# Decayed keys of two chunks by two GpSimd operations per unit, and the last output tile cut at column 384

## The chip, the cores and the metric

The kernel runs on one core of a Trainium2 chip. The metric is the device time of one execution in microseconds, taken as the median of several runs. A profiled execution of the kernel has a span (first to last instruction) and a time of its own, which is somewhat longer than the span.

## What is computed

Two stages follow each other: a block-wise linear attention with decay, and a feed-forward layer with a PReLU.

```python
# q, k, v: (4, 8, 768, 64); lam: (8,), between 0.97 and 0.99; block = 64
for b in range(nb):                       # 12 blocks
    intra = einsum('bhic,bhjc->bhij', qb, kb) * Dmask     # Dmask[i, j] = lam ** (i - j), i >= j
    intra = einsum('bhij,bhjd->bhid', intra, vb)
    inter = einsum('bhid,bhde->bhie', qb * lam_pow, kv_state)
    out[:, :, sl] = intra + inter
    kb_dec = kb * rev_pow                 # lam ** (63 - j): the decayed keys
    kv_state = lam_block * kv_state + einsum('bhsd,bhse->bhde', kb_dec, vb)

x = out as (3072, 512)
h = x @ w_in                              # (512, 2048)
g = maximum(h, 0) + alpha * minimum(h, 0)
return g @ w_out                          # (2048, 512) -> (3072, 512) float32
```

## The kernel before

**Chunks and units.** The 3072 rows are cut into six chunks of 512. A chunk holds two batches of 256 positions each; chunk `c` belongs to positions `256 * (c // 2)` and up. The attention of a chunk is done in four units: a batch (`bi`) and a half of the heads (`hh`, four heads). There are 24 units, `units[n] = (c, bi, hh)`. In chunks 0 to 3 (`c < FIRST`, `FIRST = 4`) a partition holds two neighbouring positions, and a state is carried over 128 positions. In chunks 4 and 5 the positions lie in order, each partition holds positions 128 apart (`e` = 0 and 1), and the state is carried over `N = 64`.

**A unit's steps.** Keys, and queries from unit 12 on, come as float32 by SP's DMAs (`kraw`, `qraw`), values as float16 by GpSimd's DMAs (`vh`). `cast` makes float16 copies (`qk16`). From unit 12 on, `turn_by_dma` has SP issue a transposing DMA that writes `qkT`. `decayed` multiplies the turned queries with their decay (`qdT`, L494). `key_decayed` multiplies the raw keys with theirs (`kdec`): L444 in chunks 0 to 3, L437 in chunks 4 and 5. `cluster` (L506 and on) is TensorE's part: scores (`s`, L586), new states from `kdec` and the values (L603), and the outputs of the unit before from the states (L538) and the masked scores (L558). `state` and `aged` carry the state on (L666, L677, L686).

**The feed-forward part.** `up` multiplies with `w_in` (L705), ScalarE takes the negative part (L716), VectorE joins the two (`gate`, L728), `down` multiplies with `w_out` (L738), and `store` (L749, L753) copies a 128x512 output tile from PSUM to SBUF on ScalarE and issues its DMA on ScalarE's queue. The tiles of the last chunk are made after everything else by `down_last` (L760), sixteen matmuls of 128x128 weights for each piece.

**Order.** Every engine works through its own instructions in program order; the order is written out by hand up to the second chunk's end, and then made by `weave`, which alternates the attention steps of chunk `c + 1` with the matmuls of chunk `c`. For unit `x` the four steps are `turns`, `joined`, `first_states` and `further_states`. `turns(x)` issues the transposing DMA of unit `x + 1`, at times the loads of the next chunk, and `decayed(x)`; `first_states(x)` ages the state and casts the keys of unit `x + 2` (GpSimd) and its queries (ScalarE); `further_states(x)` ends with `key_decayed(x + 2)` on GpSimd. So GpSimd's order in this part is: decayed queries of `x`, cast of keys of `x + 2`, decayed keys of `x + 2`, decayed queries of `x + 1`. Keys are decayed two units ahead of the cluster that reads them, into four buffers (`kdec`, `bufs=4`). The output tiles go to three buffers (`osb`, `bufs=3`).

Of the kernel before, what the change touches and what calls it, by code (L numbers as in the profile page):

```python
# [11 lines left out]
def kernel(  # L12
# [22 lines left out]
    ALU = mybir.AluOpType  # L35

    B, H, S, D = q.shape
# [3 lines left out]
    NC = (S // W) * 2  # L41
    NHP = H // 2
    DM = H * D
# [20 lines left out]
        out=lam_sb,  # L64
# [5 lines left out]
    raws = {}  # L70
# [4 lines left out]
    FIRST = 4  # L75
# [37 lines left out]
    w_out_sb = const.tile([128, NF, DM], fp16, name="w_out_sb")  # L113
# [50 lines left out]
    kdecay = const.tile([128, H, 2], fp32, name="kdecay")  # L164
# [8 lines left out]
    nkdecay = const.tile([128, H], fp32, name="nkdecay")  # L173
# [192 lines left out]
    def bank(slot, name):  # L366
        return ps.tile([128, CH], fp32, tag=f"b{slot}", name=name)
# [30 lines left out]
    def engine(x):  # L398
        return nc.vector if x == "V" else nc.gpsimd

    def view(t, hh):
        return t[:, ds(4 * hh, 4), :].rearrange("p h (e d) -> p e h d", e=2)
# [29 lines left out]
    def key_decayed(n, eng="G"):  # L432
        c, bi, hh = units[n]
        kr = view(raws[c, bi, "k"], hh)
        kdec = half_pool.tile([128, 2, 4, D], fp16, tag="kdec", name="kdec", bufs=4)
        if c >= FIRST:
            engine(eng).tensor_tensor(  # L437
                out=kdec.rearrange("p e h d -> p h e d"),
                in0=raws[c, bi, "k"][:, ds(4 * hh, 4), :].rearrange("p h (e d) -> p h e d", e=2),
                in1=nkdecay[:, ds(4 * hh, 4)].unsqueeze(2).unsqueeze(3).to_broadcast([128, 4, 2, D]),  # L440
                op=ALU.mult,
            )
        for e in range(2 if c < FIRST else 0):
            engine(eng).tensor_tensor(  # L444
                out=kdec[:, e],
                in0=kr[:, e],
                in1=kdecay[:, ds(4 * hh, 4), e].unsqueeze(2).to_broadcast([128, 4, D]),
                op=ALU.mult,
            )
        T.setdefault(n, {})["kdec"] = kdec  # L450
# [295 lines left out]
    def store(c, t, c0=0, n=DM):  # L746
        o_ps = O.pop((c, t))
        o_sb = o_pool.tile([128, DM], fp32, tag="osb", name="o_sb")
        nc.scalar.activation(o_sb[:, 0:n], o_ps[:, 0:n], AF.Copy)  # L749
        pb, b = c // 2, 2 * (c % 2) + t % 2  # L750
        rows = out[ds(b * S + pb * W, W), ds(c0, n)]
        rows = rows.rearrange("(j e) d -> e j d" if c < FIRST else "(e j) d -> e j d", e=2)[t // 2]
        nc.scalar.dma_start(out=rows, in_=o_sb[:, 0:n])  # L753

    def down_last(c, t, nc_parts):
        n = DM // nc_parts
        for x in range(nc_parts):
            o_ps = O[c, t] = bank(TURN[(t + x) % 3], "o_ps")
            for f in range(NF):
                nc.tensor.matmul(  # L760
                    o_ps[:, 0:n],
                    lhsT=G[c, f][:, t // 2, t % 2, :],
                    rhs=w_out_sb[:, f, ts(x, n)],
                    start=(f == 0),
                    stop=(f == NF - 1),
                )
            store(c, t, x * n, n)

# [35 lines left out]
    load_win(256, 256)  # L806
    query_decay()
    key_decayed(0, "V")
    turn(0)
    decay_mask(1)  # L810
    key_decayed(1, "G")
    fill(6)
    turned(0, "V")
# [18 lines left out]
    turned(1, "A")  # L832
    masked(0, 0)
    key_decayed(2, "G")
    masked(0, 1)
    cast(2, "k", "A")
# [424 lines left out]
        moe = ups[:1] + [x for f in range(1, NF) for x in (ups[f], downs[f - 1])] + downs[-1:]  # L1261
        weave(att, moe)
    for t in range(4):
        down_last(NC - 1, t, 1 if t < 3 else 2)


# [28 lines left out]
```

## Time and profile before

| | |
|---|---|
| median of 3 runs | 221.33 us (219.97 to 222.4) |
| profiled execution: time | 221.9 us |
| profiled execution: span | 220.1 us |
| mean granted TensorE clock | 0.988 |
| HBM read, written | 27.28 MB, 6.29 MB |
| largest groups: L705, L738 on TensorE | 98.1 and 81.2 us |
| L728 on VectorE, L716 on ScalarE | 73.2 and 59.0 us |
| all `kdec` operations on GpSimd | 30 of 128x256, 18.4 us; 8 of 128x512, 8.3 us |

PE is TensorE's matmuls, PEld its weight loads (which overlap the matmuls), DVE is VectorE, ACT ScalarE, POOL GpSimd, SP SyncE; a name with a q is that engine's issuing of DMAs. A group's row has the line, the engine and operation, what is written and read with shapes and types, the count, and then busy us, mean ns of one, idle us before, and what ended that idle time. A timeline's row begins with start and duration in us. The rows of slices cut the span into 40 equal parts; a digit is the busy share in tenths. The chain that ended last is followed back from the last instruction, at each step to what released it. Ends of matmuls are modelled, so the distance between starts says more than a duration.

### The profile page before, as it was taken

To read this page: it belongs to the slowest core of one execution; us is meant where nothing else is said; L and a number is where in the kernel's file an instruction comes from. 1 tells how busy PE (TensorE), PEld (TensorE's weight loads), DVE (VectorE), ACT (ScalarE), POOL (GpSimd) and SP (SyncE) were. 2 spreads that over 40 slices of the span, in tenths; PEclk is the share of its full clock that TensorE was granted. 3 is DMA by queue.
4 is the path that set the end of the run, shared out by engine and by line. 5 is a ranking of instruction groups with operands and counts; after the bars stand their busy time and mean duration, and the time that the engine had idled before them with its cause. 6 is when DMAs were issued, how large, how long until landed. Compare 5 with 4: busy or idle time off the path is not lost.

```text
span 220.1 us, 5893 instructions
## 1 busy us (share of the span) xinstructions
PE 211.8 (96%) x2463; PEld 114.6 (52%) x2463; DVE 127.1 (58%) x260; ACT 111.6 (51%) x209; POOL 95.9 (44%) x146
## 2 busy tenths in 40 slices
PE   8988899899999999999999999999999999999992
PEld 8777544556665545454545444444444444444461
DVE  3988577666887787464667566556755254443000
ACT  4762585744655564646664545555445434443120
POOL 7874796553998770776596243620100000000000
PEclk9999699999999999999999999999999999999998
DMA  4999999999998599299269995236011001100221
GB/s 118 244 193 232 192 159 183 202 171 196 299 229 199 85 219 118 74 184 172 74 89 217 180 229 130 64 82 71 27 51 48 17 35 48 48 38 13 95 92 53
DMA packets 71194, 28.44 MB, mean 129 GB/s; under 512 B 52080, under 2 KB 68224, under 8 KB 71168
## 3 DMA queue, kind: packets, MB, share of 16 engines
q0 software_dynamic: 26592, 8.65, 35.6%
q1 hardware_dynamic: 40800, 13.11, 31.0%
q10 hardware_dynamic: 3776, 6.31, 8.0%
q8 instruction: 19, 0.31, 0.6%
q14 instruction: 7, 0.06, 0.1%
HBM read 27.28 MB, written 6.29 MB: 153 GB/s over the span
## 4 chain that ended last, share of the span: by engine, by line
PE 91%; ACT 2%; DVE 2%; POOL 2%; issue 1%; POOLq 0%
PE h_ps L705 38%; PE o_ps L738 32%; PE o_ps L760 6%; PE acc L538 3%; PE s L586 2%; PE op_fill L380 2%; PE acc L558 2%; PE tp L466 2%; PE tp L461 1%; PE acc L603 1%; ACT qkT L392 1%; PE mk_ps L267 1%; POOL vh L83 0%; PE s L603 0%; DVE less L245 0%
## 5 line engine op out<-in xcount | busy, mean ns | idle before, releaser
L728 DVE SCALAR_TENSOR_TENSOR g<-m,oma,h_ps 128x512 f16<-128x512 f32 (+1 forms) x106 | 73.2, 696 | 64.9 <-ACT m L716 63.5
L705 PE MATMUL h_ps<-xT,w_in_sb 128*128 128x512 f16 (+1 forms) x424 | 98.1, 364 | 0.2
L716 ACT ACTIVATE m<-h_ps 128x512 f32<-128x512 f32 (+1 forms) x106 | 59.0, 557 | 57.4 <-PE h_ps L705 55.5
L738 PE MATMUL o_ps<-w_out_sb,g 128*128 128x512 f16 x320 | 81.2, 379 | 0.0
L705 PEld LDWEIGHTS <-w_in_sb 128*128 128x128 f16 x424 | 40.4, 99 | 41.1 <-issue 1.2
L738 PEld LDWEIGHTS <-g 128*128 128x128 f16 x320 | 30.9, 98 | 35.8
L749 ACT ACTIVATE o_sb<-o_ps 128x512 f32<-128x512 f32 (+1 forms) x25 | 14.5, 580 | 18.8 <-PE o_ps L760 11.1
L619 DVE TENSOR_TENSOR sm<-s,dmask 128x512 f16<-128x512 f32 x32 | 21.2, 683 | 1.8 <-PE s L586 1.8
L392 ACT ACTIVATE xT<-acc 128x512 f16<-128x512 f32 x22 | 13.1, 597 | 16.8 <-PE acc L558 9.6
L686 POOL TENSOR_TENSOR old<-R,rdecay 128x128 f32<-128x128 f16 x24 | 9.6, 408 | 26.3 <-DVE R L677 15.7
L444 POOL TENSOR_TENSOR kdec<-kraw,kdecay 128x256 f16<-128x256 f32 x30 | 18.4, 638 | 1.5 <-DMA kraw<-in_k_dram 0.8
L494 POOL TENSOR_TENSOR qdT<-qkT,nqdecay 128x512 f16<-128x512 f16 x8 | 9.3, 1165 | 21.5 <-DMA qkT<-qk 17.8
L494 POOL TENSOR_TENSOR qdT<-qkT,qdecay 128x512 f16<-128x512 f16 (+1 forms) x12 | 12.0, 1003 | 6.0 <-ACT qkT L392 3.0
L760 PE MATMUL o_ps<-w_out_sb,g 128*128 128x512 f16 (+1 forms) x80 | 14.0, 336 | 0.0
L380 PE MATMUL op_fill<-filler 128*128 128x128 f16 x122 | 10.7, 258 | 1.1 <-DVE sel L203 1.1
L538 PE MATMUL acc<-qdT,R 64*64 64x64 f16 (+1 forms) x216 | 10.9, 217 | 0.9 <-ACT R L675 0.7
L760 PEld LDWEIGHTS <-g 128*128 128x128 f16 x80 | 7.8, 98 | 6.2
L538 PEld LDWEIGHTS <-R 64*64 64x64 f16 x224 | 5.9, 104 | 9.5 <-issue 6.3
L666 DVE SCALAR_TENSOR_TENSOR R<-R,nrdecay,s 128x64 f16<-128x64 f16 x48 | 10.4, 275 | 0.0
L380 PEld LDWEIGHTS <-filler 128*128 128x128 f16 x122 | 9.3, 119 | 1.6 <-DVE sel L203 1.1
L586 PE MATMUL s<-qkT 64*64 64x128 f16 (+1 forms) x384 | 9.3, 210 | 0.9 <-issue 0.5
L558 PE MATMUL acc<-sm,vh 64*64 64x128 f16 (+1 forms) x352 | 8.5, 211 | 0.0
(98 smaller groups left out, 159.5 us busy)
## 6 DMA issues: line engine op xcount, KB each, us to landing
out_dram<-o_sb ACTq DMA_DIRECT2D x23, 256.0 KB, 2.1
kraw<-in_k_dram SPq DMA_DIRECT2D x12, 256.0 KB, 5.1
kraw<-in_k_dram SPq DMA_DIRECT2D x6, 512.0 KB, 8.0
qraw<-in_q_dram SPq DMA_DIRECT2D x10, 256.0 KB, 6.6
vh<-in_v_dram POOLq DMA_DIRECT2D x8, 256.0 KB, 9.4
w_out_sb<-in_moe_w_out_dram POOLq DMA_DIRECT2D x4, 512.0 KB, 8.3
w_in_sb<-in_moe_w_in_dram POOLq DMA_DIRECT2D x3, 512.0 KB, 10.4
qh<-in_q_dram POOLq DMA_DIRECT2D x5, 256.0 KB, 9.0
```

Source lines behind the costliest of these rows:

```text
L380: nc.tensor.matmul(t[:, 0:128], lhsT=filler, rhs=filler, start=True, stop=True)
L392: nc.scalar.activation(out, in_, AF.Copy)
L444: engine(eng).tensor_tensor(out=kdec[:, e], in0=kr[:, e], in1=kdecay[:, ds(4 * hh, 4), e].unsqueeze(2).to_broadcast([128, 4, D]), op=ALU.mult,
L494: engine(eng).tensor_tensor(out=out, in0=src, in1=(qdecay if c < FIRST else nqdecay)[:, hh].rearrange("p e h j -> p (e h) j").unsqueeze(2) ...
L538: nc.tensor.matmul(o, lhsT=before[ds(hl * 64, 64), hp, :], rhs=x, start=not own and e == 0, stop=False, skip_group_check=True,)
L619: nc.vector.tensor_tensor(out=t["sm"][hl], in0=t["s"][:, hl].rearrange("p (h x j) -> p h x j", h=2, x=2), in1=mask_of(hl, hh), op=ALU.mult,)
L705: nc.tensor.matmul(h_ps[:, 0:n] if bi is None else h_ps[:, 0:n].rearrange("p (e j) -> p e j", e=2), lhsT=w_in_sb[:, gi, ts(f, 128)], rhs=x ...
L716: nc.scalar.activation(m[:, 0:n], HP[c, f, bi][:, 0:n], AF.Relu, scale=-1.0)
L728: nc.vector.scalar_tensor_tensor(out=g, in0=mv, scalar=oma[:, f : f + 1], in1=hv, op0=ALU.mult, op1=ALU.add)
L738: nc.tensor.matmul(O[c, t], lhsT=G[c, f][:, t // 2, t % 2, :], rhs=w_out_sb[:, f, :], start=(f == 0), stop=(f == NF - 1),)
L749: nc.scalar.activation(o_sb[:, 0:n], o_ps[:, 0:n], AF.Copy)
L760: nc.tensor.matmul(o_ps[:, 0:n], lhsT=G[c, f][:, t // 2, t % 2, :], rhs=w_out_sb[:, f, ts(x, n)], start=(f == 0), stop=(f == NF - 1),)
```

## The change

It has two parts. In `key_decayed`, chunks 4 and 5 no longer have an operation of their own over 128x512 elements; all chunks use the loop over `e`, two operations of 128x256 per unit, and the decay is chosen by chunk. In chunks 4 and 5 both halves are multiplied by the same decay. In `down_last`, the widths of the pieces are handed over; the last tile goes out as 384 and 128 columns, where it was 256 and 256.

```diff
         kdec = half_pool.tile([128, 2, 4, D], fp16, tag="kdec", name="kdec", bufs=4)
-        if c >= FIRST:
-            engine(eng).tensor_tensor(
-                out=kdec.rearrange("p e h d -> p h e d"),
-                in0=raws[c, bi, "k"][:, ds(4 * hh, 4), :].rearrange("p h (e d) -> p h e d", e=2),
-                in1=nkdecay[:, ds(4 * hh, 4)].unsqueeze(2).unsqueeze(3).to_broadcast([128, 4, 2, D]),
-                op=ALU.mult,
-            )
-        for e in range(2 if c < FIRST else 0):
+        for e in range(2):
+            decay = kdecay[:, ds(4 * hh, 4), e] if c < FIRST else nkdecay[:, ds(4 * hh, 4)]
             engine(eng).tensor_tensor(
                 out=kdec[:, e],
                 in0=kr[:, e],
-                in1=kdecay[:, ds(4 * hh, 4), e].unsqueeze(2).to_broadcast([128, 4, D]),
+                in1=decay.unsqueeze(2).to_broadcast([128, 4, D]),
                 op=ALU.mult,
             )
...
-    def down_last(c, t, nc_parts):
-        n = DM // nc_parts
-        for x in range(nc_parts):
+    def down_last(c, t, pieces):
+        c0 = 0
+        for x, n in enumerate(pieces):
             o_ps = O[c, t] = bank(TURN[(t + x) % 3], "o_ps")
             for f in range(NF):
                 nc.tensor.matmul(
                     o_ps[:, 0:n],
                     lhsT=G[c, f][:, t // 2, t % 2, :],
-                    rhs=w_out_sb[:, f, ts(x, n)],
+                    rhs=w_out_sb[:, f, ds(c0, n)],
                     start=(f == 0),
                     stop=(f == NF - 1),
                 )
-            store(c, t, x * n, n)
+            store(c, t, c0, n)
+            c0 += n
...
-        down_last(NC - 1, t, 1 if t < 3 else 2)
+        down_last(NC - 1, t, (DM,) if t < 3 else (DM - 128, 128))
```

## The prediction

> **What bounds the kernel now.** I read the page first, for the busy engine and for the chain of waits.
>
> ```profile
> span 220.1 us, 5893 instructions
> ...
> PE 211.8 (96%) x2463; PEld 114.6 (52%) x2463; DVE 127.1 (58%) x260; ACT 111.6 (51%) x209; POOL 95.9 (44%) x146
> ...
> POOL 7874796553998770776596243620100000000000
> ...
> PE 91%; ACT 2%; DVE 2%; POOL 2%; issue 1%; POOLq 0%
> ```
>
> TensorE works for 211.8 of 220.1 us, and 91% of the chain that ended last is TensorE's. GpSimd (POOL) has 44%, all in the first three quarters. So an edit on GpSimd counts only if it makes TensorE wait, and an edit at the very end counts in full, since nothing comes after it.
>
> The first edit touches units 16 to 23 (chunks 4 and 5). Their decayed keys are written between 100.4 and 140.9 us. From 95 us on, the list of who waited for whom has not one row for TensorE. How far ahead GpSimd runs is seen in its timeline, start and duration in us, beside the chain in order of time:
>
> ```profile
> 107.27 0.40 POOL L686 TENSOR_TENSOR old<-R,rdecay 128x128 f32<-128x128 f16 x1 [4.67 <-DVE R L677]
> ...
> 108.18 1.04 POOL L437 TENSOR_TENSOR kdec<-kraw,nkdecay 128x512 f16<-128x512 f32 x1
> 109.18 1.16 POOL L494 TENSOR_TENSOR qdT<-qkT,nqdecay 128x512 f16<-128x512 f16 x1
> ...
> 115.34 1.04 POOL L437 TENSOR_TENSOR kdec<-kraw,nkdecay 128x512 f16<-128x512 f32 x1
> ...
> 118.41 1.16 POOL L494 TENSOR_TENSOR qdT<-qkT,nqdecay 128x512 f16<-128x512 f16 x1 [0.26 <-DMA qkT<-qk]
> ```
>
> ```profile
> 109.95 0.12 PE s L603 x12
> ...
> 115.66 0.18 PE acc L538 x8
> 115.85 0.13 PE s L586 x16
> 115.97 0.12 PE s L603 x12
> ```
>
> L603 reads the decayed keys. The keys of unit 16, written from 100.44 to 101.5, are read at 109.95, and those of unit 17, written from 108.18 to 109.2, at 115.97: margins of 8.5 and 6.7 us. The next unit's keys are written at 110.85 and read at 123.65, so the margin grows. The decayed queries of unit 16, which follow the keys of unit 17 on GpSimd, end at 110.3 and are read at 115.66 (L538): 5.3 us, the smallest margin of anything that stands behind a changed operation and is made by GpSimd itself.
>
> The second edit is at the end. Here the timeline of the last tile:
>
> ```profile
> 212.48 0.60 ACT L749 ACTIVATE o_sb<-o_ps 128x512 f32<-128x512 f32 x1 [2.86 <-PE o_ps L760]
> ...
> 214.22 0.38 ACT L749 ACTIVATE o_sb<-o_ps 128x256 f32<-128x256 f32 x1 [1.15 <-PE o_ps L760]
> 214.64 0.34 ACTq L753 DMA_DIRECT2D out_dram<-o_sb  x1
> 215.97 0.38 ACT L749 ACTIVATE o_sb<-o_ps 128x256 f32<-128x256 f32 x1 [1.36 <-PE o_ps L760]
> 216.38 0.34 ACTq L753 DMA_DIRECT2D out_dram<-o_sb  x1
> ```
>
> After the last matmul come a copy of 0.38 us, a gap of 0.03, the output's DMA, 1.7 us from issue to landing (216.38 to 218.1), and 2.0 us of closing work up to 220.1.
>
> **Part one: keys by two operations.** Removed: eight operations of 128x512. Added: sixteen of 128x256, of the form that the first four chunks have on the same line pair:
>
> ```profile
> L444 POOL TENSOR_TENSOR kdec<-kraw,kdecay 128x256 f16<-128x256 f32 x30 | 18.4, 638 | 1.5 <-DMA kraw<-in_k_dram 0.8 <-ACT kdecay L292 0.6
> ...
> L437 POOL TENSOR_TENSOR kdec<-kraw,nkdecay 128x512 f16<-128x512 f32 x8 | 8.3, 1041 | 0.0
> ```
>
> The group of 30 has a median of 616 ns, a lowest of 604 and a highest of 848. With the median, one unit costs 2 x 0.616 - 1.041 = 0.19 us more; from below 2 x 0.604 - 1.049 = 0.16, from above 2 x 0.848 - 1.034 = 0.66. I take 0.19, because after 60 us all operations of this form lie within 605 to 619 ns. The sum over eight units is 1.5 us of GpSimd (1.3 to 5.3). Nothing can be gained: the one operation had no wait before it (idle 0.0) and its result is not read sooner.
>
> On the path I cost it at nothing, and the cover is the margins above. Queued behind a unit's keys on GpSimd are the decayed queries of the unit before, the cast of the next unit's keys and, twice, two loads of the values (0.9 us each of issuing). Each of them shifts by 0.2 us, in the tightest stretch (107.3 to 117.2, three changed units, no idle time) by up to 0.6. Against that stand 5.3 us or more. The cast of keys also releases SP's transposing DMA. For units 18 and 19 the queries' cast on ScalarE ends 1.6 and 3.1 us after GpSimd's cast, so this DMA doesn't move; for unit 17 GpSimd had been idle for 4.67 us just before, so the shift of unit 16's keys is used up there. Even where such a DMA moves by 0.2, its median landing of 4.1 us ends about 3 us before TensorE asks for it (unit 20: lands by 135.5, read at 138.7). The new wait of TensorE, for the second half of each unit's keys, ends with the margin of the whole. If the cover were gone, the price would be the 0.2 us of each unit, 1.5 in all, with the dearest rows 5.3.
>
> A row of the trace speaks for the dear end: at 8.4 us VectorE and GpSimd both run this operation, and the two then take 839 and 848 ns, against 426 and 614 apart. In chunks 4 and 5 VectorE's operations (L728, L628, L666) each take one operand from PSUM, and the changed operation kept to 1034 to 1049 ns among them. [...]
>
> **Part two: 384 and 128 columns.** TensorE: the 512-column tiles come 3.46 us apart for 16 matmuls (209.02 to 212.48), 0.216 each; the 256-column pieces 1.74, 0.109 each. 384 columns lie half way, 0.1625, so 2.60 us for sixteen. For 128 columns the nearest rows are:
>
> ```profile
> 18.81 0.95 PE L380 MATMUL op_fill<-filler 128*128 128x128 f16 x14
> ...
> 54.83 0.39 PE L461 MATMUL tp<-ident,k 128*128 128x128 f16 x4
> ```
>
> and, for the weights of this very step (busy us, mean ns, idle us):
>
> ```profile
> L760 PEld LDWEIGHTS <-g 128*128 128x128 f16 x80 | 7.8, 98 | 6.2
> ```
>
> A single one lasts 0.219, so the fourteen started (0.95 - 0.22) / 13 = 0.056 us apart, and the four, each with weights of its own, (0.39 - 0.22) / 3 = 0.057. That is in the proportion of the columns, though a weight load lasts 98 ns: the loads overlap. So sixteen take 0.90 us, and both pieces 3.50 against 3.49 before: TensorE ends 0.01 us later. From above, with 98 ns each, they would take 1.57, which is 0.68 more.
>
> [...] The trace shows 56 in both streams, the one with changing weights being only four long.
>
> ScalarE: the first piece's copy starts at 212.48 + 2.60 = 215.08 and lasts 0.49 (half way between 0.597 and 0.384; the 384-column exponential of L277 takes 0.489). Its DMA is issued from 215.60 to 215.94. The second piece is ready at 215.98, so ScalarE is free just in time; at worst it loses some 0.03. The last copy, 128 columns, takes 0.28 by the same line (0.597 - 3 x 0.107; L675 takes 0.274 for 128 columns): 0.10 us less than 0.38.
>
> The output's DMA: the table of transfers has
>
> ```profile
> out_dram<-o_sb ACTq DMA_DIRECT2D x23, 256.0 KB, 2.1
> ...
> out_dram<-o_sb ACTq DMA_DIRECT2D x2, 128.0 KB, 1.7
> ```
>
> 0.4 us for 128 KB, so 0.2 for the 64 KB that the last transfer loses: 1.5 us. Bounds: 1.7 if it is all fixed, 1.3 if the slope doubles. The 192 KB of the first piece land at 215.60 + 1.9 = 217.5, before the last at 216.29 + 1.5 = 217.8, so they are hidden by 0.3 us; taken as 256 KB (2.1) still by 0.1.
>
> Sum: +0.01 (TensorE) + 0 (keys) - 0.10 (copy) - 0.2 (landing) = -0.3 us, with bounds from -0.5 to +0.6. The profiled execution took 221.9, 1.8 more than its span; that would give 221.6. The median of the three runs is 0.57 below it, so I subtract from 221.33: 221.0.
>
> **The rivals.**
> - *The last sixteen matmuls are paced by their weight loads.* Place: the 128-column piece, from about 215.1 us. It decides as soon as a 98 ns load can't run under a 56 ns matmul. Price +0.68 - 0.3: about +0.4, so 221.7, slower than before. For it: the row of weight loads; against it: the two streams above. Chance 0.09, and the page's 81 ns (+0.1, 221.4) another 0.06.
> - *The transfer is all fixed cost.* Only the copy's 0.10 is gained: 221.2. For it: 1.7 against 2.1 is a small part of either, and medians are rounded. Chance 0.12.
> - *GpSimd's delay reaches TensorE.* If each unit's 0.19 to 0.66 us were paid, +1.5 to +5.3, 222.5 to 226.3. It decides where the shift passes 5.3 us, or 3 us through SP's transposes; 0.6 are expected. Chance 0.05.
>
> **How the numbers follow.** The forecast has the remaining 0.68, and its time is 221.0. All cases but the last lie within 0.5 us of the time before, less than the scatter of its three runs (219.97 to 222.4). So the range is set by that scatter, moved by the forecast at the low end (219.7), and at the high end (222.4) with 0.2 for the paced matmuls and the cheap end of the GpSimd case: 222.6. A measurement of this kernel can tell about 1%, 2.2 us, from no change. Only the dear part of the GpSimd case (0.04) passes it; scatter of a median of few runs adds some 0.05 on each side. Faster 0.05, within 1% 0.86, slower 0.09.
>
> **What would show it.** Right: GpSimd's keys at 0.60 to 0.63 us, sixteen of them; no wait of TensorE from 95 us on; the copies at the end of 0.49 and 0.28 us, starts 0.9 us apart; a landing near 1.5 us; a span near 219.8. Wrong: a wait of L603, L586 or L538 for GpSimd or for a transpose; keys of 0.8 us; starts of the two last copies 1.3 us or more apart (weights); an unchanged 1.7 us landing.

## The result, and the profile after

The changed kernel took 220.27 us (median of 20 runs, 219.52 to 221.08), the kernel before 220.88 (20 runs, 219.97 to 222.4). The ratio is 0.9963 with a 95% interval of 0.9948 to 0.9979: a gain of 0.5 to 1.1 us, 0.8 in the middle; the two medians lie 0.6 apart. The time lies in the forecast range (219.7 to 222.6) and the sign is as predicted, but the gain is two to three times the 0.3 us that was worked out. Ratios here and below leave out executions at a much lower granted clock (0.56 to 0.85), of which there were three, none of them in this comparison.

The two profiled executions differ by more, 218.0 against 220.1 us of span, and most of that is not the change. The page after:

```profile
span 218.0 us, 5901 instructions
...
PE 209.7 (96%) x2463; PEld 112.9 (52%) x2463; DVE 126.9 (58%) x260; ACT 111.4 (51%) x209; POOL 97.4 (45%) x154
...
POOL 7874797655988680875597352720200000000000
```

and the stretch from 20 to 40 us, which the change doesn't touch, first after and then before (busy us and count of each engine, then the granted clock of TensorE, DMA share, GB/s):

```profile
20.00:40.00 20.00, 18.20 (x209) 10.26 (x207) 13.51 (x24) 12.98 (x26) 14.99 (x23) 1.00 1.32 189
```

```profile
20.00:40.00 20.00, 18.56 (x168) 10.23 (x166) 12.71 (x22) 11.97 (x25) 14.35 (x23) 0.91 1.32 188
```

Before, TensorE had a granted clock of 0.91 in this stretch (half speed for 3.4 us of it, by the clock's records), after, 1.00. It got through 168 matmuls there before and 209 after. This comes and goes from run to run in both kernels (six of the changed kernel's 20 executions have a mean clock of 0.992, the others 0.998 to 1.0). So I compare from a place behind it: the start of ScalarE's copy of the third tile of the last chunk, 212.48 us before and 211.01 after. That part, 1.47 us, is start-up scatter and not the change: the first changed operation, unit 16's keys, already starts 1.48 us earlier (98.96 against 100.44). What is left, with differences taken before rounding:

| from the third tile's copy | before | after | difference |
|---|---|---|---|
| start of the last copy | 3.49 | 3.56 | +0.07 |
| its length with the gap up to the DMA | 0.41 | 0.31 | -0.11 |
| DMA, issue to landing | 1.70 | 1.57 | -0.13 |
| closing work, last landing to end | 2.01 | 1.57 | -0.45 |
| sum | 7.62 | 7.01 | -0.62 |

The first three rows are the predicted effect, -0.17 us where -0.3 was worked out. The fourth, the largest, was not predicted at all. The first three can be read from the timeline after (start, duration):

```profile
211.01 0.60 ACT L743 ACTIVATE o_sb<-o_ps 128x512 f32<-128x512 f32 x1 [2.86 <-PE o_ps L754]
...
213.61 0.49 ACT L743 ACTIVATE o_sb<-o_ps 128x384 f32<-128x384 f32 x1 [2.00 <-PE o_ps L754]
214.13 0.34 ACTq L747 DMA_DIRECT2D out_dram<-o_sb  x1
214.57 0.28 ACT L743 ACTIVATE o_sb<-o_ps 128x128 f32<-128x128 f32 x1 [0.47 <-PE o_ps L754]
214.88 0.34 ACTq L747 DMA_DIRECT2D out_dram<-o_sb  x1
```

The fourth is in the closing instructions, which all have the line of the program's last call (L1290 before, L1285 after). The two views of that line, GpSimd's rows alone (lowest, median and highest ns, first and last start):

```profile
L1290 POOLq DRAIN  x3: 107/178/2668, 153.7 to 219.7; - x3
...
L1290 POOLq EVENT_SEMAPHORE_RANGE_CLEAR  x1: 157/157/157, 219.2 to 219.2; - x1
```

```profile
L1285 POOLq DRAIN  x3: 45/98/2678, 152.6 to 217.7; - x3
...
L1285 POOLq EVENT_SEMAPHORE_RANGE_CLEAR  x1: 158/158/158, 217.6 to 217.6; - x1
```

A drain is an instruction of the closing work; GpSimd clears the semaphores and then drains once more. Before, the drain starts 0.5 us after the clearing; after, about 0.2. To the nanosecond, the clearing ended at 219.351 and the drain ran from 219.689 to 219.867 before; after, 217.710 and 217.744 to 217.789. A gap of 0.338 us became 0.034, and a drain of 0.178 became 0.045. The drain names no semaphore in the trace, so it waits for no other engine by what is recorded. In the trace of before an 8 KB transfer on queue q14, whose kind the profile's page calls "instruction", runs from 219.21 to 219.66, and the drain starts 24 ns behind it. That this transfer causes the gap is not borne out: in the trace of after the like transfer runs from 217.59 to 218.13 and outlasts a drain that isn't held.

GpSimd's keys did what was expected of their time:

```profile
L438 POOL TENSOR_TENSOR kdec<-kraw,nkdecay x16: 609/612/618, 99.0 to 139.8; 128x256 f16<-128x256 f32 x16
```

The list of who waited for whom has no row for TensorE's matmuls (PE) from 95 us on, as before. The rows for its weight loads (PEld), 4.6 us in all and 5.0 before, name an issue, VectorE or TensorE itself, and none names GpSimd.

### The profile page after: what moved, and what is told of

It is laid out like the page before. It is cut to its first block, busy times and chain, and to the rows that moved or that the text cites. A ratio compares the mean times of both kernels' runs of the same rounds, so it can differ in the third digit from the quotient of the medians.

```text
span 218.0 us, 5901 instructions
## 1 busy us (share of the span) xinstructions
PE 209.7 (96%) x2463; PEld 112.9 (52%) x2463; DVE 126.9 (58%) x260; ACT 111.4 (51%) x209; POOL 97.4 (45%) x154
## 4 chain that ended last, share of the span: by engine, by line
PE 91%; ACT 2%; DVE 2%; issue 2%; POOL 2%; ACTq 0%; POOLq 0%
PE h_ps L699 37%; PE o_ps L732 32%; PE o_ps L754 6%; PE acc L532 3%; PE s L580 2%; PE op_fill L380 2%; PE acc L552 2%; PE tp L460 2%; PE tp L455 1%; PE acc L597 1%; ACT qkT L392 1%; PE mk_ps L267 1%; ACT xT L392 1%; POOL vh L83 0%; ACT m L710 0%
## 5 line engine op out<-in xcount | busy, mean ns | idle before, releaser
L699 PE MATMUL h_ps<-xT,w_in_sb 128*128 128x512 f16 (+1 forms) x424 | 96.7, 359 | 0.5 <-DVE g L722 0.2
L699 PEld LDWEIGHTS <-w_in_sb 128*128 128x128 f16 x424 | 39.6, 98 | 40.6 <-issue 1.4
L732 PEld LDWEIGHTS <-g 128*128 128x128 f16 x320 | 30.9, 98 | 35.8
L743 ACT ACTIVATE o_sb<-o_ps 128x512 f32<-128x512 f32 (+2 forms) x25 | 14.5, 580 | 18.8 <-PE o_ps L754 11.0
L754 PE MATMUL o_ps<-w_out_sb,g 128*128 128x512 f16 (+2 forms) x80 | 14.0, 336 | 0.0
L754 PEld LDWEIGHTS <-g 128*128 128x128 f16 x80 | 7.2, 98 | 6.9
L438 POOL TENSOR_TENSOR kdec<-kraw,nkdecay 128x256 f16<-128x256 f32 x16 | 9.5, 612 | 0.0
```

Of the source, the lines that this page charges most:

```text
L438: engine(eng).tensor_tensor(out=kdec[:, e], in0=kr[:, e], in1=decay.unsqueeze(2).to_broadcast([128, 4, D]), op=ALU.mult,)
L699: nc.tensor.matmul(h_ps[:, 0:n] if bi is None else h_ps[:, 0:n].rearrange("p (e j) -> p e j", e=2), lhsT=w_in_sb[:, gi, ts(f, 128)], rhs=x ...
L732: nc.tensor.matmul(O[c, t], lhsT=G[c, f][:, t // 2, t % 2, :], rhs=w_out_sb[:, f, :], start=(f == 0), stop=(f == NF - 1),)
L754: nc.tensor.matmul(o_ps[:, 0:n], lhsT=G[c, f][:, t // 2, t % 2, :], rhs=w_out_sb[:, f, ds(c0, n)], start=(f == 0), stop=(f == NF - 1),)
```

## The experiments

Three theories came up in turn. **A**: GpSimd is held once at a fixed place of its instruction stream; the keys' eight more instructions move that place from the closing work to where GpSimd idles anyway. **B**: the closing work is shorter because the last transfer is smaller. **C**, from a surprise on the way: SP is held in the same manner. The expectations call A's hold a fetch, and one of them speaks of fetched blocks: both are suppositions of the author, which no run shows. All closing numbers below are from the profiled execution of each kernel, one for each; ratios are to the kernel before, timed beside it. The kernels with one and with four memsets, the kernel before with one SP instruction, and the changed kernel with two were profiled once and have no ratio.

**One part alone.** The two parts of the diff, each without the other.

> Only the last tile is cut at 384; the keys are as before, so GpSimd has as many instructions as before. Theory A (a fetch for GpSimd during the closing work held the kernel before; its place depends on GpSimd's instruction count): last landing to end stays 2.0 us, GpSimd's last two instructions come after a gap of about 0.34 us, and the gain is that of copy and landing alone, about 0.15 to 0.2 us against before (ratio about 0.999). Theory B (the closing work got shorter because the last transfer is smaller): last landing to end 1.5 us, gain 0.6 us, ratio about 0.997.

> Only the keys by two operations; the last tile is 256 and 256. Theory A: eight more GpSimd instructions, last landing to end 1.5 us instead of 2.0, gain about 0.45 us (ratio about 0.998), TensorE's part up to the last tile unchanged. Theory B: closing work 2.0 us, no gain (ratio 1.000). In both: no wait of TensorE for GpSimd after 95 us.

With the tail alone: ratio 0.9994 (0.9971 to 1.0017), third tile's copy to last landing 5.44 us as in the changed kernel, and the closing work 2.01 as before, with a gap of 0.323 on GpSimd. With the keys alone: ratio 0.9976 (0.9952 to 1.0), 5.61 to the landing as before, and closing work 1.57 with a gap of 0.034. So -0.17 us belongs to the tail and -0.45 to the keys, and the two add up to the whole -0.62. This rests on the traces: the ratios' intervals reach about 0.5 us to each side, and can't tell the two parts from each other. B is out, by the closing work of the two traces. The tail that was meant as the gain is the smaller part; the keys, costed at nothing, are the larger.

**Instructions that do nothing.** Is it the split of the keys, or only the number of GpSimd's instructions?

```diff
+    pad = const.tile([128, 1], fp32, name="pad")
...
         T.setdefault(n, {})["kdec"] = kdec
+        for _ in range(1 if c >= FIRST else 0):
+            nc.gpsimd.memset(pad, 0.0)
```

> The kernel before with one 128x1 memset on GpSimd after each of the eight units' keys of chunks 4 and 5; nothing reads it. Theory A: the count of instructions alone decides, so last landing to end 1.5 us and a gain of about 0.45 us, as with the keys by two operations. Rival (the split of the keys itself does it, by timing): 2.0 us and no gain.

> The changed kernel with the same eight memsets, sixteen GpSimd instructions more than before in all. Theory A: if a fetch is met only when the last instructions stand just behind the end of a fetched block, the closing work stays at 1.5 us and the time that of the changed kernel (within 0.1 us); if the place matters in a finer way, 2.0 us and 0.45 us slower than the changed kernel. Rival (the gain comes from the changed kernel's parts, not from the count): as the changed kernel.

The first was a miss: ratio 1.0003 (0.9984 to 1.0022), closing work 1.86 us. But the gap had moved. It was 0.034 ahead of the drain and 0.334 behind it. The count explains it: these memsets each wait on GpSimd's own semaphore, and nine separate waiting instructions fell away (44 before, 35 here). With eight memsets more and nine waits less, GpSimd had one instruction less, and it was held one instruction later in its closing sequence. The second, the changed kernel with the same memsets (seven more than before in all), stayed at 1.56 us, with a ratio of 0.9979 (0.9958 to 1.0), and the tail's total of 7.00 was that of the changed kernel.

So the count was set cleanly, by memsets without waits behind GpSimd's last work, in the kernel before:

```diff
+    pad = const.tile([128, 16], fp32, name="pad")
...
+    for i in range(8):            # 1 and 4 in the other two
+        nc.gpsimd.memset(pad[:, i : i + 1], 0.0)
     for t in range(4):
         down_last(NC - 1, t, 1 if t < 3 else 2)
```

> The kernel before with eight 128x1 memsets on GpSimd behind its last decayed queries, each into a column of its own, with no wait; nothing reads them. This makes GpSimd's instructions eight more without a change of anything else (in the earlier kernel with memsets, nine separate waits fell away, so it had one instruction less, not eight more). Theory A (count decides): last landing to end 1.56 us, no gap between GpSimd's last clearing of semaphores and its last drain, gain 0.45 us as with the keys by two operations. Rival (the split of the keys decides): 2.0 us with the gap of 0.34, no gain.

> One such memset. Theory A: the gap of 0.34 us is met one instruction earlier, between GpSimd's drain and the clearing of the semaphores, and last landing to end is still 1.9 to 2.0 us. Rival: gap where it was before.

> Four such memsets. Theory A: the gap moves ahead of GpSimd's first closing instructions, where GpSimd waits for SP anyway, so it is hidden in part or whole: last landing to end 1.56 us, or up to 1.9 if the fetch begins only when the last semaphore arrives. Rival: 2.0 us.

Eight memsets: closing work 1.57 us, ratio 0.9974 (0.9951 to 0.9997), the gain of the keys without any change of the keys. Four: 1.57. One: 1.88, with the gap of 0.335 between GpSimd's drain and the clearing, one instruction earlier than before. Measured on the trace of each, in instructions against the kernel before:

```
GpSimd instructions                   gap of GpSimd in its closing work       landing to end, us
-1 (before, memsets at the keys)      0.334 behind the last drain             1.86
 0 (before; tail alone)               0.338, 0.323 ahead of the last drain    2.01, 2.01
+1 (one memset at the end)            0.335 ahead of the clearing             1.88
+4 (four memsets at the end)          none                                    1.57
+7 (changed, memsets at the keys)     none                                    1.56
+8 (eight at the end; keys; changed)  none                                    1.57
```

In the views, eight memsets first, then one, the clearing follows 0.1 us behind the drain, or 0.5 us:

```profile
L1293 POOLq DRAIN  x2: 45/72/98, 217.3 to 217.6; - x2
...
L1293 POOLq EVENT_SEMAPHORE_RANGE_CLEAR  x1: 157/157/157, 217.4 to 217.4; - x1
```

```profile
L1293 POOLq DRAIN  x2: 45/76/107, 217.7 to 218.4; - x2
...
L1293 POOLq EVENT_SEMAPHORE_RANGE_CLEAR  x1: 157/157/157, 218.2 to 218.2; - x1
```

The place moves by one instruction for each that is added: A is shown as far as the place goes. Counted in the traces, the held instruction is GpSimd's 197th in each row that has a gap. In the changed kernel the 197th is an operation on decayed queries at 143.51 us, and it does start late: 0.38 us behind the wait ahead of it, where the same operation took 0.09 before. So the hold is still there, at a place where TensorE doesn't wait for it. The case of none added is dearer than its neighbours by 0.14 us, mostly because its last drain takes 0.178 instead of 0.045; why, was not tried.

**The last copy on VectorE.** In the changed kernel's chain of waits ScalarE's DMA issue stands just ahead of the last copy:

```profile
213.61 0.50 ACT o_sb L743
214.11 0.02 issue
214.13 0.34 ACTq L747
214.47 0.04 issue
214.51 0.02 ACTq L743
214.53 0.04 issue
214.57 0.28 ACT o_sb L743
```

The last matmul ended at 214.47; in the other tiles ScalarE follows within 0.04 us, here after 0.10, since it was issuing the 384 columns' DMA until 214.47 and then took one more wait. The edit:

```diff
-        nc.scalar.activation(o_sb[:, 0:n], o_ps[:, 0:n], AF.Copy)
+        last = c == NC - 1 and t == 3 and c0 > 0
+        copy_on("V" if last else "A", o_sb[:, 0:n], o_ps[:, 0:n])
...
-        nc.scalar.dma_start(out=rows, in_=o_sb[:, 0:n])
+        (nc.sync if last else nc.scalar).dma_start(out=rows, in_=o_sb[:, 0:n])
```

> The changed kernel with the last copy (128 columns) on VectorE and its DMA on SP's queue. In the changed kernel ScalarE was free only after the first piece's copy, DMA issue and a semaphore, 0.07 us after TensorE's end as worked out. If that wait is real: from the third tile's copy to the last landing 5.37 us or less instead of 5.44, and a gain of 0.05 to 0.1 us; GpSimd's count is that of the changed kernel, so the closing work stays at 1.56. Rival: VectorE's copy is slower than 0.28 us or SP's issue dearer than 0.34, and it is no gain.

The rival was right on the landing: 5.46 us against 5.44. VectorE began its copy 0.09 us after the last matmul, took 0.29, and SP's issue was 0.02 longer. Yet the closing work, expected to stay at 1.56, fell to 1.14 us, and the ratio was 0.9906 (0.9881 to 0.9931), the best of all. Where SP had taken 0.48 us from the wait that the last landing ends to its next wait, whose semaphore had long arrived, it now took 0.06. The trace explains 1.03 us of the gain over the kernel before, a ratio of 0.995; the rest of the 0.9906 is not explained. It comes from five runs with mean clocks of 0.998 to 1.0, while seven of the 17 runs of the kernel before stood at 0.992.

**SP's count.** Was that SP's own issue of the last DMA, or once more one instruction more?

```diff
+    nc.sync.wait_ge(apart, 1)     # long reached; twice in the third kernel
     for t in range(4):
```

> The changed kernel with one more instruction on SP, a wait on a semaphore that has long had its value, behind SP's last transposing DMA. In the changed kernel SP takes 0.48 us from the wait that the last landing ends to the next one, whose semaphore had nothing left to come; in the kernel with the last copy on VectorE that step took 0.06. Theory C (SP too is held once at a fixed place of its instruction stream, so that one instruction more puts it ahead of the last landing, where it is hidden): closing work 1.12 to 1.15 us instead of 1.57, gain 0.4 us on the changed kernel, ratio to before about 0.994. Rival D (the step is shorter because the last DMA was issued by SP): 1.57 us, as the changed kernel.

> The kernel before with the same one SP instruction. Theory C: SP's step 0.06 to 0.08 us instead of 0.47; GpSimd's gap of 0.34 stays, so closing work about 1.6 us instead of 2.0. Rival D: 2.0 us.

> The changed kernel with two such SP instructions. Theory C: the hold moves one more instruction ahead, and is hidden there too: closing work 1.12 to 1.15 us. Rival D: 1.57 us.

With one SP instruction the changed kernel took 219.23 us, ratio 0.9926 (0.9899 to 0.9953); SP's step is 0.09 and the closing work 1.17. The first and last start of SP's two waits, in the changed kernel and then with one instruction more:

```profile
L1285 SPq EVENT_SEMAPHORE  x2: 28/28/28, 216.5 to 216.9; - x2
```

```profile
L1287 SPq EVENT_SEMAPHORE  x2: 28/28/28, 216.5 to 216.6; - x2
```

With two, 0.07 and 1.14. In the kernel before, one makes SP's step 0.09, leaves GpSimd's gap at 0.337, and the closing work is 1.61; that run's last landing took 1.95 us instead of 1.70, so its time says nothing more. C holds, D is out.

**Neither part of the change.** The kernel before, with four memsets on GpSimd and one SP wait.

> Neither part of the change: the kernel before with four memsets behind GpSimd's last work and one SP wait that is already met. Theories A and C: no hold on either engine, closing work 1.12 to 1.15 us; third tile's copy to the end 5.61 + 1.13 = 6.74 us, against 7.62 before and 7.01 with the change; ratio to before about 0.996, as good as the changed kernel or better by some 0.25 us. Rival D: 1.57 us, 7.18.

Ratio 0.9929 (0.9902 to 0.9956): five instructions that compute nothing gained at least as much as the change (0.9963, 0.9948 to 0.9979; the intervals just overlap). Its profile was taken while TensorE had a granted clock of 0.56, so of it only the closing work is used, 1.15 us, and not the tail's total of 6.74. That is 0.86 us less than before, a ratio of 0.996; the timed one comes from five runs, and its surplus is not explained. The versions with the best ratios are the changed kernel with one SP instruction or with the last copy on VectorE; their intervals overlap with each other and with this one.

## Why the prediction was right, and where it was wrong

**What bounds the kernel.** Right. GpSimd works 1.5 us more (97.4 against 95.9), and TensorE waits for it nowhere from 95 us on, where the changed operations stand.

**Keys, their price.** Right: 0.612 us each where 0.616 was taken, sixteen of them, and margins that hid it. The dear end (0.848, both engines at it at once) was not met; the highest was 0.618.

**Keys, "Nothing can be gained".** Wrong, and the step that failed. It looked at waits and readers alone, and took the 2.0 us behind the last landing as a constant. The instruction count moved it: -0.45 us, shown by the keys alone and by eight idle memsets in their place.

**TensorE's last pieces.** Right, and closely: the starts in the trace are 0.1625 us apart for 384 columns and 0.056 for 128, both as taken. The groups by shape have this row for the sixteen (busy us, mean ns, idle us):

```profile
L754 PE MATMUL o_ps<-w_out_sb,g 128*128 128x128 f16 x16 | 1.1, 219 | 0.0
```

(1.06 - 0.219) / 15 = 0.056, each with weights of its own, whose loads take 98 ns. The rival of matmuls paced by weight loads is out for these sixteen. No run shows the 81 ns that the prediction gives a chance of 0.06, nor the +0.1 us drawn from it: this stream kept to 56 ns through all sixteen.

**The copy.** 0.277 us as taken (0.28), but it began 0.07 later than before where 0.01, at worst some 0.03 more, was allowed. The worked-out time left out one further wait of ScalarE, behind its DMA issue.

**The landing.** The right mechanism with the wrong size: -0.13 us instead of -0.2. The slope came from medians of 2.1 and 1.7 us; the third tile's own 256 KB landed in 2.03 us before, which would have given 0.16 for 64 KB. The rival of a fully fixed transfer is out as well: the last 64 KB on ScalarE's queue landed in 1.57 to 1.58 us in all five versions that have them, the last 128 KB in 1.70 to 1.71 in seven of eight (1.95 in the eighth).

So the tail gave 0.17 of the 0.3 us expected, and a mechanism that no rival held gave 0.45 more. The time fell within the range, but most of the gain came from where none was expected: that the total gain was no smaller than forecast is luck.

**What stays open.** What the hold is, a fetch or something else, is not shown. The traces show a fixed count, 197 for GpSimd and 80 for SP, and an 8 KB transfer on q14 that follows each hold seen in the closing work. It starts 0.69 to 0.72 us behind the start of GpSimd's held instruction in all five traces that have the gap (220.38 us before). Where the gap is gone, one such transfer more runs at 144 to 156 us instead (at 242 in the profile at 0.56 of the clock). Behind SP's held instruction one starts 0.63 to 0.82 us later (219.21 before, the one that ends 24 ns ahead of GpSimd's drain). But no q14 transfer ends with the hold in every trace: in the kernel before with one SP instruction, GpSimd's gap of 0.337 stands between 217.68 and 218.01, and the q14 transfers run from 216.21 to 216.52 and from 218.71 on. What the engines wait for in the hold itself stays open.

## What to carry to other kernels

The end of a kernel, from its last landing to its last instruction, is not a constant (here 2.01 to 1.14 us): compare its steps between the two traces before giving a gain of half a microsecond to the edit itself. An edit that adds or takes instructions on an engine can have an effect that lies in their number alone (here four memsets took the closing work from 2.01 to 1.57 us), and the control for it is cheap: the same number of idle instructions in the unchanged kernel. Where two profiled executions differ early, at a place that the edit doesn't touch, measure from behind it.

## What the runs showed of the hardware that was not expected

GpSimd lost 0.30 to 0.45 us, and SP 0.40 to 0.43, at one place of their closing sequences. The place is set by how many instructions stand ahead of it: counted in the traces, the held one is GpSimd's 197th and SP's 80th. Moved ahead of the closing work, the hold cost nothing that the traces show: the closing work fell to 1.57 and 1.14 us. The transfers on q14 that follow the holds were 8 KB each; those on q8, of the same kind, were 16 KB.
